# Recurrent attention and a four-branch network on one core: the order of VectorE's queue in the last group, and of two attention steps

## The chip, the core and the metric

The kernel runs on one core of a Trainium2 chip. Its time is the device time of one execution in microseconds (us); the number that counts is the median of the runs of one kernel. A profile comes from one execution of its own, so the time of that execution stands beside it.

## What is computed

Two parts follow each other. The first is a gated linear recurrence over 768 positions, for 4 batches and 8 heads of 48 numbers:

```python
for t in range(S):
    state = alpha[:, :, t, :, None] * state + np.einsum('bhd,bhe->bhde', k[:, :, t], v[:, :, t])
    y[:, :, t] = np.einsum('bhd,bhde->bhe', q[:, :, t], state)
```

Its result, seen as x with 3072 rows of 384 numbers, goes through four branches of two layers, weighted with normalised probabilities p:

```python
for e in range(E):                      # E = 4, hidden width F = 1024
    h = np.maximum(x @ w1[e], 0.0)
    out += p[:, e:e + 1] * (h @ w2[e])
```

All of it is in 32-bit floats.

## The kernel before

**Attention.** The recurrence is computed in blocks of 128 positions. There are 24 units, (block, batch) with the block as the slow index. For a unit, `attention(u)` is a Python generator; each `yield` ends a step, and the steps are issued one at a time between other work. Its steps, called beats: three steps that transpose alpha, keys and queries on TensorE (`tp`); three levels of a doubling scheme, in which ScalarE copies queries into `qb` (`copy_q`, line 307) and keys (L325), and VectorE multiplies queries and keys by decays (L314, L326); the fourth query copy, with the start of `near` on VectorE (L359); 64 score products on TensorE (`sc`, L333), taken into `near` by VectorE (L343); the last levels; the products of the far half (`far`, L388) and of two more levels; ScalarE's copies of `far` (L401) and of `near` (L405) into `lat`; then the result `yps` (L425), which multiplies the past state and `lat`, and its copy by ScalarE into `x_raw` (L441, or L445 in the last group); then the transposes of the last keys (`tp` again) with ScalarE's copy of them (L450); last, the update of the state `st` (products L454, VectorE L462 and L463) and the load of the values `v` two units ahead on the SP queue. Units of the last block (the last four) need no state update.

**The two layers.** The 24 units form seven groups: groups 0 and 6 (`LAST`) hold two units, the others four. A group's rows are columns of the first layer: 512 for four units, 256 for two. For each branch e of a group, `up` makes eight tiles of the hidden layer, and `down` the second layer. From group 1 on the products are split: a number is written as a sum of parts of fewer bits (top, low and a combination of them), and three products of parts stand for one product. In groups 2 to 6 a tile of `up` is nine matmuls into two PSUM tiles, `one` (six) and `two` (three). ScalarE takes `one` out with a factor (`t`, L538); VectorE adds `two` (L540, "the sum"); `hidden_parts` then has ScalarE make the top part with the ReLU (L563, "top"), VectorE the low part L (L565) and from both the part D (`make_dif`, L573) in two halves: the first at once, the second put into the list `later`. The generator of a tile waits in the list `finish`, and is run after the matmuls of the next tile are issued and before that tile's L538 and L540. `down` in these groups takes two units at a time: 48 products of 384 columns, first all that use top and L (32), then those that use D (16); one entry of `later` is made after every fifth product. Each unit's two sums are accumulated by VectorE (L641, the first branch by ScalarE, L639). The PSUM tiles `one`, `two` and the sums share four buffers; `tp`, `yps` and the state's products share two others; `t` has two buffers.

**The order.** [...]The tasks are (group, branch), and groups 5 and 6 take turns within each branch. Within a task, `advance` moves a clock of estimated TensorE time by the cost of each tile or product; `deal` gives each attention step a due time on that clock, and a step is issued when the clock has reached it. A unit's steps lie between a beginning and an end, two spaces long, so that two units overlap; a space is 11.5 in group 1, and 27 to 34 later. The 17 steps stood at equal distances (`BEATS = 17`). The last unit of a group ends 6.0 (`MARGIN`) before the second layer in which `split_x` takes its result. The two units of group 0 are issued by a list written out by hand. Weights are split into parts in the first two groups (L223 to L229), stored to memory on the POOL queue (L230), and loaded again on SP (L194).

Of the kernel before, what the change touches and what calls it, by code (L numbers as in the profile page):

```python
# [10 lines left out]
F32 = mybir.dt.float32  # L11
F32R = mybir.dt.float32r
# [8 lines left out]
def kernel(  # L21
# [124 lines left out]
    BEATS = 17  # L146
# [121 lines left out]
    def attention(u):  # L268
# [143 lines left out]
        yps = ps.tile([P, KC, P], F32, name="yps", tag="w")  # L412
        for c in range(KC):


            if c < 2:
                now = [[(2 * c + j // 2, j % 2, (0, HD + TAIL)[j % 2], 2 * QUAD * (j % 2))
                        for j in range(4)]]
                turns = ([(True, now[0])] if cb > 0 else []) + [(False, now[0])]
            else:  # L420
                turns = [(True, [(p, 0, 0, QUAD) for p in range(NP)])] if cb > 0 else []
                turns += [(False, [(p, i, QUAD + TAIL * i, 0) for p in range(NP)]) for i in range(2)]
            for n, (past, turn) in enumerate(turns):
                for j, (p, i, in_v, in_st) in enumerate(turn):
                    nc.tensor.matmul(  # L425
                        yps[QUAD * j:QUAD * (j + 1), c, :],
                        lhsT=flat_st[:, p, in_st:in_st + QUAD] if past
                        else flat_v[:, p, in_v:in_v + QUAD],
                        rhs=QT[:, p, :] if past else lat[:, 2 * p + i, :],
                        start=(n == 0), stop=(n == len(turns) - 1))  # L430
        gi, slot = place[cb, b]
        if slot == 0:
            if gi == 0:
                xTs[gi] = work.tile([P, 3, KC, NT], F32R, name="xT", bufs=1)
                xraws[gi] = xTs[gi][:, 2].bitcast(F32)
            elif gi < LAST:
                xraws[gi] = work.tile([P, KC, NT], F32, name="x_raw", bufs=1)
            else:
                xraws[gi] = []
        if gi < LAST:  # L440
            nc.scalar.copy(out=xraws[gi][:, :, slot * P:(slot + 1) * P], in_=yps)  # L441
        else:

            xraws[gi].append(AT)
            nc.scalar.copy(out=AT[:, :KC, :], in_=yps)  # L445
        yield

        if cb < NCB - 1:
            KB = AT
            nc.scalar.copy(out=KB, in_=turned(lambda p: KT[:, p, :]))  # L450
            yield
# [42 lines left out]
    def up(gi, e, fc, slots=None):  # L494
# [31 lines left out]
        else:  # L526
# [7 lines left out]
            while finish:  # L534
                for _ in finish.popleft():
                    pass
            t = work.tile([P, NT], F32, name="t")[:, :n]
            nc.scalar.activation(out=t, in_=one, func=ACT.Copy, scale=FINE)  # L538
            if split2(gi, e):
                nc.vector.tensor_add(t, t, two)  # L540
                finish.append(hidden_parts(t, parts))
            else:
                nc.vector.tensor_add(whole, t, two)  # L543
                finish.append(rectified(whole))
# [16 lines left out]
    def hidden_parts(x, parts):  # L561
        top, low, dif = parts
        nc.scalar.activation(out=top, in_=x, func=ACT.Relu, scale=TRIM)  # L563
        yield
        nc.vector.scalar_tensor_tensor(out=low, in0=x, scalar=0.0, in1=top.bitcast(F32),  # L565
                                       op0=ALU.max, op1=ALU.subtract)

        n = x.shape[-1]
        make_dif(*(part[:, :n // 2] for part in parts))
        later.append([part[:, n // 2:] for part in parts])  # L570
# [9 lines left out]
    def down(gi, e, slots, between):  # L580
# [14 lines left out]
        for n, (part, i, fc) in enumerate(steps):  # L595
# [7 lines left out]
            if later and n % 5 == 4:  # L603
                make_dif(*later.popleft())
# [54 lines left out]
    def deal():  # L659
# [14 lines left out]
        for gis in [*([gi] for gi in range(1, LAST - 1)), [LAST - 1, LAST]]:  # L674
# [6 lines left out]
            for k in range(n):  # L681
# [5 lines left out]
                events += [(begin + (end - begin) * (j + 1) / BEATS, u, run) for j in range(BEATS)]  # L687
# [103 lines left out]
```

## Time and profile before

| what | us |
|---|---|
| median of 12 runs | 1084.27 |
| lowest and highest of them | 1082.58, 1085.38 |
| the profiled execution | 1085.0 |
| its span on the core | 1083.2 |
| busy: TensorE, its weight loads, VectorE, ScalarE | 1058.0, 898.9, 779.7, 564.4 |

In the lines of the profile, L607 is a line of the kernel, PE is TensorE's matmuls, PEld its weight loads (which run beside the matmuls), DVE VectorE, ACT ScalarE, and SP and POOL the engines whose queues issue most transfers. `t<-one` means that the instruction writes tile `t` from tile `one`. In the timeline a line has its start, its duration, the engine, the line, the operation, the tiles, the shape and how many instructions were merged; a bracket at the end gives the idle time of the engine before it and what ended that. In the lines of waits, the numbers are the total, how often and the longest. The median time of one instruction is longer than the distance to the next one where instructions overlap in an engine's pipeline.

### The profile page before, as it was taken

The page shows a single profiled execution, that of the slowest core. Times are in us where ns is not written, and L with a number is a line of the kernel's source. Part 1 is how long each engine was busy: PE and PEld are TensorE (multiplying, and loading weights), DVE is VectorE, ACT ScalarE, POOL GpSimd, SP SyncE. Part 2 cuts the span into 40 slices and gives each one's busy share as a digit, 9 for nine tenths or more (in the row PEclk, how much of TensorE's full clock was granted, in tenths as well). Part 3 has the DMA queues.
Part 4 walks back from the last instruction along what each step waited for, and adds up shares of the span by engine and source line. Part 5 has one row for each costly group of instructions (what it writes and reads, how often), then busy time and mean ns, then how long its engine had stood idle before and what let it go on. Part 6 is the DMA issues. An engine that isn't in the chain of part 4 may idle for free.

```text
span 1083.2 us, 21627 instructions
## 1 busy us (share of the span) xinstructions
PE 1058.0 (98%) x8460; PEld 898.9 (83%) x8460; DVE 779.7 (72%) x1743; ACT 564.4 (52%) x1202; POOL 32.9 (3%) x71
## 2 busy tenths in 40 slices
PE   8889899999999999999999999999999999999998
PEld 8766677676777798898898898888989889898987
DVE  5578678657557869778878777986887965756565
ACT  5786776664757555546546445565464442323232
POOL 2000000000000100000000000000000000000000
PEclk9999999999999999999999999999999999999999
DMA  8597679796696968658759559577594444444530
GB/s 124 156 327 232 210 244 377 291 329 234 213 311 221 400 203 286 269 165 310 252 175 359 204 185 351 181 265 262 148 357 180 186 190 175 175 180 170 202 163 30
DMA packets 158838, 251.67 MB, mean 232 GB/s; under 512 B 120112, under 2 KB 135344, under 8 KB 136208
## 3 DMA queue, kind: packets, MB, share of 16 engines
q1 hardware_dynamic: 149600, 208.82, 55.8%
q0 software_dynamic: 5760, 41.29, 9.7%
q8 instruction: 67, 1.10, 0.4%
q10 hardware_dynamic: 3376, 0.17, 0.3%
q14 instruction: 35, 0.29, 0.1%
HBM read 207.79 MB, written 42.47 MB: 231 GB/s over the span
## 4 chain that ended last, share of the span: by engine, by line
PE 78%; DVE 9%; ACT 7%; issue 3%; DMA 2%; SPq 0%; ACTq 0%; DVEq 0%
PE ops L607 25%; PE one L531 19%; PE ops L611 9%; PE two L531 9%; PE sc L333 5%; PE yps L425 3%; PE tp L265 2%; ACT qb L307 2%; DVE t L540 2%; PE one L523 2%; DVE hT L565 2%; ACT hT L563 2%; PE sps L454 1%; PE far L388 1%; DVE near L343 1%
## 5 line engine op out<-in xcount | busy, mean ns | idle before, releaser
L607 PE MATMUL ops<-w,hT 128*128 128x384 f32 x1728 | 318.3, 340 | 2.0 <-DVE acc L641 1.5
L607 PEld LDWEIGHTS ops<-w,hT 128*128 128x128 f32 x1728 | 298.7, 188 | 7.8 <-DVE acc L641 2.8
L531 PE MATMUL one<-xT,w 128*128 128x512 f32 x960 | 253.7, 399 | 1.1 <-DMA w<-kept 0.7
L531 PEld LDWEIGHTS one<-xT,w 128*128 128x128 f32 x960 | 175.8, 188 | 42.4 <-issue 2.4
L538 ACT ACTIVATE t<-one 128x512 f32<-128x512 f32 (+1 forms) x192 | 106.1, 553 | 162.0 <-PE one L531 145.7
L307 ACT COPY qb<-QT 64x256 f32<-64x256 f32 x336 | 136.6, 406 | 70.0 <-DVE QT L288 35.7
L563 ACT ACTIVATE hT<-t 128x512 fp32r<-128x512 f32 (+1 forms) x160 | 94.3, 590 | 122.5 <-DVE t L540 121.3
L565 DVE SCALAR_TENSOR_TENSOR hT<-t,hT 128x512 fp32r<-128x512 f32 (+1 forms) x160 | 102.3, 639 | 75.5 <-ACT hT L563 74.1
L531 PE MATMUL two<-xT,w 128*128 128x512 f32 x480 | 136.2, 392 | 0.0
L611 PE MATMUL ops<-hT 128*128 128x384 f32 x384 | 135.6, 497 | 0.0
L573 DVE SCALAR_TENSOR_TENSOR hT<-hT 128x256 fp32r<-128x256 f32 (+1 forms) x320 | 117.4, 395 | 5.5
L540 DVE TENSOR_TENSOR t<-t,two 128x512 f32<-128x512 f32 (+1 forms) x160 | 100.7, 629 | 23.6 <-PE two L531 11.7
L531 PEld LDWEIGHTS two<-xT,w 128*128 128x128 f32 x480 | 90.2, 188 | 19.8
L611 PEld LDWEIGHTS ops<-hT 128*128 128x128 f32 x384 | 70.0, 192 | 40.5 <-issue 1.6
L343 DVE COPY_PREDICATED near<-masks,sc 128x256 f32<-128x256 uint8 x144 | 77.1, 535 | 17.9 <-PE sc L333 14.8
L314 DVE TENSOR_TENSOR QT<-QT,dec 128x256 f32<-128x256 f32 x144 | 60.7, 422 | 33.1 <-ACT qb L307 32.7
L333 PEld LDWEIGHTS sc<-qb,KT 128*64 128x64 f32 x2304 | 72.5, 138 | 9.2 <-issue 7.1
L333 PE MATMUL sc<-qb,KT 128*64 128x64 f32 x2304 | 76.7, 223 | 0.2 <-ACT qb L307 0.2
L641 DVE SCALAR_TENSOR_TENSOR acc<-ops,p_all,acc 128x384 f32<-128x384 f32 x82 | 49.5, 613 | 29.1 <-PE ops L607 13.7
L326 DVE TENSOR_TENSOR KT<-KT,dec 128x256 f32<-128x256 f32 x144 | 60.3, 419 | 2.6 <-PE tp L265 2.6
L325 ACT COPY KT<-KT 128x256 f32<-128x256 f32 x144 | 59.8, 416 | 3.1
L543 DVE TENSOR_TENSOR hT<-t,two 128x512 f32<-128x512 f32 x32 | 22.0, 688 | 35.6 <-ACT t L538 26.1
(88 smaller groups left out, 972.3 us busy)
## 6 DMA issues: line engine op xcount, KB each, us to landing
w<-kept SPq DMA_DIRECT2D x144, 1152.0 KB
kept<-w POOLq DMA_DIRECT2D x32, 1152.0 KB, 7.6
hT<-in_moe_w_dram SPq DMA_DIRECT2D x32, 384.0 KB
w<-in_moe_w_dram SPq DMA_DIRECT2D x48, 128.0 KB
ra<-in_alpha_dram SPq DMA_DIRECT2D x23, 192.0 KB
rk<-in_k_dram SPq DMA_DIRECT2D x23, 192.0 KB
rq<-in_q_dram SPq DMA_DIRECT2D x23, 192.0 KB
out_dram<-acc POOLq DMA_DIRECT2D x18, 192.0 KB, 5.8
```

Of the source, the lines that this page charges most:

```text
L307: nc.scalar.copy(out=qb[rows, :, i, :].rearrange("p a (b r) -> p a b r", r=m), in_=qv[rows])
L314: nc.vector.tensor_mul(qv, qv, spread(dv[:, :, :, 0], m))
L333: nc.tensor.matmul(out[HALF * s:HALF * (s + 1), 2 * p:2 * p + 2, :], lhsT=KTs[li][:, p, HALF * s:HALF * (s + 1)], rhs=qbs[li][:, p, :, QUA ...
L343: nc.vector.copy_predicated(near.rearrange("p a (b two r) -> p a b two r", two=2, r=m)[:, :, :, 1, :], mk.unsqueeze(1).broadcast_to([P, H, ...
L531: nc.tensor.matmul(out, lhsT=w[:, part, kc], rhs=x_part(gi, part, kc), start=(part == terms[0] and kc == 0), stop=(part == terms[-1] and k ...
L538: nc.scalar.activation(out=t, in_=one, func=ACT.Copy, scale=FINE)
L540: nc.vector.tensor_add(t, t, two)
L563: nc.scalar.activation(out=top, in_=x, func=ACT.Relu, scale=TRIM)
L565: nc.vector.scalar_tensor_tensor(out=low, in0=x, scalar=0.0, in1=top.bitcast(F32), op0=ALU.max, op1=ALU.subtract)
L573: nc.vector.scalar_tensor_tensor(out=dif, in0=top.bitcast(F32), scalar=1 / 4096.0, in1=low.bitcast(F32), op0=ALU.mult, op1=ALU.subtract)
L607: nc.tensor.matmul(sums[i][part // 2], lhsT=h[:, part], rhs=w, start=(fc == 0 and part != 1), stop=(fc == FCH - 1 and part != 0))
L611: nc.tensor.matmul(sums[i][0], lhsT=h[:, 2].bitcast(F32), rhs=w, start=(fc == 0), stop=(fc == FCH - 1))
```

## The change

There are five edits.

1. The beats become a list: eleven at distances of 0.055 of a unit's time (before, 1/17 = 0.0588), then 0.69, 0.75, 0.80, 0.87, 0.94 and 1.0 (before, 0.706, 0.765, 0.824, 0.882, 0.941 and 1.0).
2. From unit 2 on, the transposes of the last keys and ScalarE's copy of them (`turn_keys`) are issued one step before the result and its copy (`result`) instead of one step after. Units of the last block have an empty step in the place of `turn_keys`, so their result moves from step 15 to step 16 and the load of `v` from step 16 to step 17.
3. In the last group, only the top part of the tile before is issued ahead of a tile's L538 and L540. Its L (L565) is issued behind that L540.
4. In the last group no half of D is made in `up`: the whole part, 256 columns, goes into `later`.
5. `down` makes one entry of `later` after every fourth product instead of every fifth.

```diff
-    BEATS = 17
+    BEATS = [*(0.055 * (j + 1) for j in range(11)), 0.69, 0.75, 0.8, 0.87, 0.94, 1.0]
...
+        def result():
+            yps = ps.tile([P, KC, P], F32, name="yps", tag="w")
...
+        def turn_keys():
+            if cb < NCB - 1:
+                nc.scalar.copy(out=AT, in_=turned(lambda p: KT[:, p, :]))
+
+
+        for step in (turn_keys, result) if u >= half else (result, turn_keys):
+            step()
+            yield
 
         if cb < NCB - 1:
             KB = AT
-            nc.scalar.copy(out=KB, in_=turned(lambda p: KT[:, p, :]))
-            yield
...
-            while finish:
-                for _ in finish.popleft():
+
+            ends_first = gi < LAST
+            for steps in finish:
+                for _ in steps if ends_first else [next(steps)]:
                     pass
+            ahead = [] if ends_first else list(finish)
+            finish.clear()
             t = work.tile([P, NT], F32, name="t")[:, :n]
             nc.scalar.activation(out=t, in_=one, func=ACT.Copy, scale=FINE)
             if split2(gi, e):
                 nc.vector.tensor_add(t, t, two)
+                for steps in ahead:
+                    next(steps, None)
                 finish.append(hidden_parts(t, parts))
...
         n = x.shape[-1]
-        make_dif(*(part[:, :n // 2] for part in parts))
-        later.append([part[:, n // 2:] for part in parts])
+        at = n // 2 if n == NT else 0
+        if at:
+            make_dif(*(part[:, :at] for part in parts))
+        later.append([part[:, at:] for part in parts])
...
-            if later and n % 5 == 4:
+            if later and n % 4 == 3:
                 make_dif(*later.popleft())
...
-                events += [(begin + (end - begin) * (j + 1) / BEATS, u, run) for j in range(BEATS)]
+                events += [(begin + (end - begin) * beat, u, run) for beat in BEATS]
```

## The prediction

> **What bounds the kernel now.** I read the page first (TensorE busy 98% of the span), then the chain that ended last (78% TensorE, 9% VectorE, 7% ScalarE), then TensorE's waits, then the stretches and the timeline where the chain leaves TensorE. The busy time by stretch, columns PE, PEld, DVE, ACT, POOL, then clock, DMA share, GB/s:
>
> ```profile
> 60.00:150.00 90.00, 80.91 (x858) 61.61 (x857) 66.02 (x151) 64.29 (x145) 4.80 (x9) 0.96 0.72 234
> 150.00:180.00 30.00, 29.09 (x179) 21.06 (x178) 24.82 (x49) 20.38 (x43) 3.22 (x6) 1.00 1.04 396
> 180.00:700.00 520.00, 518.33 (x4154) 430.48 (x4156) 385.05 (x838) 287.15 (x593) 15.01 (x28) 1.00 0.73 260
> 700.00:903.00 203.00, 201.85 (x1735) 179.82 (x1725) 158.09 (x361) 104.04 (x223) 2.16 (x4) 1.00 0.61 220
> 903.00:1083.00 180.00, 174.74 (x984) 159.67 (x983) 112.33 (x263) 51.11 (x114) 0.00 (x0) 1.00 0.42 165
> ```
>
> From 180 to 903 us TensorE has under 3 us without work: nothing that only moves VectorE's or ScalarE's work can gain there. It lacks 9 us at 60–150 and 5 us at 903–1083. What it waits for (total, times, longest):
>
> ```profile
> PE yps L425 <- ACT lat L405: 8.5, 6, 3.5
> PE far L388 <- ACT qb L307: 4.6, 4, 1.6
> PE ops L607 <- DVE acc L641: 1.5, 2, 0.9
> ```
>
> The two long waits on `lat` lie at 77.7 and 120.8, and a stretch at half clock follows each (the 0.50 column), with TensorE busy all through it:
>
> ```profile
> 80.84:84.25 3.41, 3.41 (x34) 1.99 (x22) 2.96 (x6) 3.17 (x8) 0.00 (x0) 0.50 0.31 107
> 125.21:128.62 3.41, 3.41 (x28) 2.03 (x21) 1.96 (x6) 1.51 (x4) 0.00 (x0) 0.50 0.88 341
> ```
>
> The other place is the last group's first layer, four times eight tiles of 256 columns. Its timeline:
>
> ```profile
> 903.90 0.88 PE L531 MATMUL one<-KT,w 128*128 128x256 f32 x6
> ...
> 904.98 0.88 PE L531 MATMUL one<-KT,w 128*128 128x256 f32 x6
> ...
> 907.37 0.41 DVE L540 TENSOR_TENSOR t<-t,two 128x256 f32<-128x256 f32 x1
> ...
> 907.82 0.42 ACT L563 ACTIVATE hT<-t 128x256 fp32r<-128x256 f32 x1 [0.88 <-DVE t L540]
> ...
> 908.14 0.37 ACT L538 ACTIVATE t<-one 128x256 f32<-128x256 f32 x1
> 908.27 0.42 DVE L565 SCALAR_TENSOR_TENSOR hT<-t,hT 128x256 fp32r<-128x256 f32 x1 [0.48 <-ACT hT L563]
> 908.56 0.77 PEld L531 LDWEIGHTS one<-KT,w 128*128 128x128 f32 x6 [0.30 <-ACT t L538]
> ...
> 908.73 0.29 DVE L573 SCALAR_TENSOR_TENSOR hT<-hT 128x128 fp32r<-128x128 f32 x1
> 908.94 0.41 DVE L540 TENSOR_TENSOR t<-t,two 128x256 f32<-128x256 f32 x1
> ...
> 913.26 8.59 PE L607 MATMUL ops<-w,hT 128*128 128x384 f32 x48
> ```
>
> Unhindered, TensorE starts a tile every 904.98 − 903.90 = 1.08 us. VectorE's sums (L540) come every 908.94 − 907.37 = 1.57 us, because sum, top (L563), L (L565), D (L573) and the next sum follow one another. After three tiles PSUM is full and TensorE keeps VectorE's pace.
>
> **What the Trainium skill says.** *Perfetto Trace Analysis*, Identifying the Most-Contended Engine: matmul busy time is a poor measure of the distance to the limit. The trace agrees: PE reads 98% while the last group's tiles run at 1.57 instead of 1.08 us; so I count starts, not busy time. *TensorE: Matmul & The Clock Gate*, Part 1: an idle window of about 3.4 us halves the clock until a busy window has passed. The trace agrees, with 3.41 us at 0.50 twice, after waits of 2.73 and 3.50 us. *VectorE: DVE Perf Modes*, the section on the fixed latency of SBUF operations: (N+151)/0.96 ns for an fp32 tensor-tensor operation, 424 ns at N = 256; the trace has 415 (L540) and 425 (L565). I use the trace.
>
> **The change, part by part.**
>
> *Last group, first layer.* VectorE's queue becomes sum(k), L(k−1), sum(k+1); D leaves. The loop that remains is sum(k) → top(k) → t(k+1), behind top(k) in ScalarE's queue → sum(k+1): 907.82 − 907.37 = 0.45, then 908.14 − 907.82 = 0.32, then eviction to sum 0.42 (903.80 to 904.22 at the stage's first tile): 1.19 us. The new wait: t(k+1) also needs the `t` buffer that L(k−1) reads. L follows a sum after about 0.345 us (nine 256-column pieces in 3.11 us at 890.00) and is heard by ScalarE after 0.45, so t starts 0.80 after the sum: 1.22 us. I take 1.22. That is above 1.08, but two tiles of PSUM lie between: t(k) starts at 903.80 + 1.22k and frees its bank 0.42 later (908.14 → 908.56), so tile k may start at 901.78 + 1.22k and wants 902.84 + 1.08k. They meet at k = 7.6: only the second layer waits, 0.06 us. The layer takes 8 × 1.08 + 0.06 = 8.70 instead of 913.26 − 902.84 = 10.42, and 4 × 1.72 = **6.9 us** go. Bounds: 2.6 (loop 1.40) to 7.1 (no stop).
>
> *D in the second layer.* Eight pieces of 256 replace two sets of eight of 128, at about 0.345 against 2 × 0.21 us each. The last L ends some 2.6 us after the second layer begins, so the pieces are through 8 × 0.345 = 2.8 later, at 5.4. The first is needed at product 32 (32 × 0.179 = 5.7; 48 products take 8.59), then one per product; the eighth, emitted before product 31 behind one accumulation (0.62), is due at 7.0 and done at about 6.5. TensorE hides it: 0, at most 0.3 each. In groups 2 to 5 the same pieces come at every fourth product instead of every fifth: seven instead of five stand ahead of the first accumulation, 0.7 us, and its bank is wanted 18 products = 3.2 us later. 0, −1 to +1 us.
>
> *Keys ahead of the result, and the beats.* Four transposes and a ScalarE copy (0.58 us) go ahead of the result's products and their copy (0.48), which come a beat later; the state update keeps its beat. The keys need VectorE's last L326, done at 76.1 where the turn comes at 77.4, and at 119.4 where it comes at 120.4. In the first attention group two units overlap at a beat of 23/17 = 1.35 us, and ScalarE, 64 of 90 us busy, is late for each copy.
> At 77.4 the copy of `near` moves ahead of one first-layer tile's work (0.38 + 0.84), so `lat` is ready at 79.2 instead of 80.4. But the next unit's score products now follow the result at once and need a query copy that ScalarE ends at 83.3 either way. They end at 83.9 and one product behind them at 84.25; before, both were through at 86.3: 2.1 us.
> At 120.4 the earlier first beats put a query copy into ScalarE's idle 1.9 us at 116.7, `lat` is ready at 122.9, and the scores end at 126.6, a product later 126.95, at full clock; before, that point was reached at 132.0: 5.0 us. At 99.5 the wait of 0.96, some 1.2 with what follows, goes. Sum 8.3. Behind it, at 150–180, VectorE (24.8 of 30) and the DMA (1.04) are full; their work is issued earlier too, but not all will follow. I take **6**. Bounds: 0, since ScalarE does the same work, and 12.5 = 1.6 (far) + 7.4 (lat) + 2 × 3.41/2 (clock).
> In later groups the result is about 2 us or more behind its copies already; one wait (0.87 at 804.97) goes: **1.0**, bounds −1 and 2. The loads of `v` for the last two units leave one beat (3 us) later on SP, over 20 us ahead of use: 0. The result must be there for the split of x: 0.06 of two spaces of 27–34 us plus a margin of 6 leaves 9 us. 0.
>
> *Sum:* 6.9 + 6 + 1 = 13.9. The profiled run took 1085.0 (span 1083.2 and 1.8 around it), 0.7 above the median of 1084.27. Against the median: 1084.3 − 13.9 = **1070.4**.
>
> **Rivals.**
> 1. *ScalarE sets the pace at 60–150 in any order*: TensorE no longer waits for `lat` but for the query copies behind it. For it: ScalarE is never idle at 77.7–84. Against: it idles 1.9 us at 116.7 and at 127. Only the last group's gain and 1 us stay: 1084.3 − 7.9 = 1076.4.
> 2. *The last group's loop is longer*, 1.40: the two hand-overs from L and top to t add up. Tile 8 then waits until 912.6; each layer saves 0.65: 1084.3 − 2.6 − 7 = 1074.7.
> 3. *Slower*: the D pieces and denser first beats delay VectorE's accumulations, so that each second half of a second layer waits for its banks. There are 16 such places in groups 2–5. It decides once the delay passes the 3.2 us of slack; at 1.1 us each it costs 17.6: 1084.3 − 13.9 + 17.6 = 1088.0. For it: two such waits today. Against: they total 1.5 us, and the added backlog is 0.7.
> 4. *All waits at 60–150 go*, with the clock: 1084.3 − 6.9 − 12.5 = 1064.9.
>
> **How the numbers follow.** Forecast 0.56, rivals 0.20, 0.12, 0.04, 0.06; rivals 1 and 2 together (2.6 + 1) with 2 us lost to the beats elsewhere, 0.02: 1082.7, which is no change. The range leaves out the slower one and the far end of rival 4: 1065.0 to 1078.5, where 1078.5 is rival 1 with −1 us elsewhere and a few tenths more. A measurement of this kernel can tell about 0.2% (2.2 us) from no change. All other cases but the slower one lie beyond that: faster 0.94, same 0.02, slower 0.04.
>
> **What would show it.** First layers of the last group at about 8.7 us with L540 every 1.2 us; no waits of the result on `lat` above 1.5 us; no half-clock stretches at 80–130; 180–700 unchanged within 2 us. I am wrong if TensorE's wait only moves to the scores (L333) or to the key transposes (L265), or if waits on the accumulations (L641) grow past 5 us.

## The result and the profile after

| | before | after |
|---|---|---|
| median, us | 1084.95 (32 runs) | 1073.26 (8 runs) |
| lowest and highest, us | 1082.58, 1087.15 | 1072.18, 1075.76 |
| the profiled execution and its span, us | 1085.0, 1083.2 | 1074.11, 1072.3 |

The ratio of after to before is 0.9897, with a 95% interval of 0.9888 to 0.9906. The median fell by 11.7 us, the profiled span by 10.9; 13.9 were forecast. The line numbers of the changed kernel are higher: L308 is the copy of queries, L334 the scores, L389 `far`, L402 and L406 the copies into `lat`, L428 the result, L540 the first layer's products, L551, L553, L578, L580 and L590 are t, sum, top, L and D, L624 and L628 the second layer's products, L658 the accumulation, and L248 the split of x.

The busy times by stretch of the changed kernel (the columns are those of the prediction's table); the last two stretches are moved along with the work:

```profile
60.00:150.00 90.00, 84.80 (x897) 67.10 (x896) 70.44 (x162) 71.41 (x158) 5.56 (x11) 1.00 0.80 263
150.00:180.00 30.00, 27.88 (x195) 19.91 (x194) 24.02 (x50) 18.01 (x40) 2.68 (x5) 0.94 1.01 361
180.00:700.00 520.00, 518.98 (x4215) 433.91 (x4214) 387.97 (x844) 287.41 (x592) 14.99 (x28) 1.00 0.74 262
700.00:895.00 195.00, 190.85 (x1607) 171.06 (x1597) 151.50 (x345) 98.87 (x213) 2.16 (x4) 1.00 0.60 214
895.00:1073.00 178.00, 173.47 (x999) 161.56 (x997) 107.88 (x232) 54.24 (x115) 0.00 (x0) 1.00 0.42 167
```

At 60–150 TensorE lacks 5.2 us where it lacked 9.1, and its clock is full. At 150–180 something new has come: 2.1 us without work instead of 0.9, and a clock of 0.94. And 700–895 now lacks 4.2 us where the like stretch lacked 1.2. TensorE's waits in the changed kernel (total, times, longest) say on what:

```profile
PE ops L624 <- DVE acc L658: 4.4, 4, 1.9
PE far L389 <- ACT qb L308: 3.2, 3, 1.6
PE yps L428 <- ACT lat L406: 3.1, 4, 1.5
PE sc L334 <- ACT qb L308: 2.6, 3, 1.2
PE one L540 <- DVE xT L248: 1.3, 1, 1.3
...
PE one L540 <- DMA w<-kept: 0.8, 1, 0.8
```

The result's wait on `lat` fell from 8.5 to 3.1 us. The scores (L334), the accumulations (L658) and the split of x (L248) wait longer than before.

To see where time came from, I took the start of the same product on TensorE in both traces and subtracted:

| first product of | before | after | saved so far |
|---|---|---|---|
| group 0, branch 3, second layer | 157.80 | 150.73 | 7.07 |
| group 1, branch 0, first layer | 171.90 | 165.13 | 6.78 |
| group 1, branch 1, first layer | 220.60 | 215.84 | 4.77 |
| group 4, branch 1, second layer | 762.23 | 754.58 | 7.66 |
| group 4, branch 2, first layer | 783.31 | 777.41 | 5.90 |
| group 6, branch 0, first layer | 902.84 | 897.34 | 5.49 |
| the end | 1083.22 | 1072.35 | 10.88 |

So 7.1 us are won by 150 us, 2.3 of them are lost again by 216 us, 0.7 net come by 897 (2.9 won by 755, of which 1.8 go in one layer and 0.4 later), and 5.4 in the last stretch. The four first layers of the last group took 9.03 us each, where they had taken 10.42, 10.42, 10.71 and 10.43: 1.39 + 1.39 + 1.68 + 1.40 = 5.9 us.

The last group's first layer in the timeline of the changed kernel (a bracket gives the engine's idle time before the line, and what ended it):

```profile
1053.26 0.42 DVE L553 TENSOR_TENSOR t<-t,two 128x256 f32<-128x256 f32 x1 [0.76 <-ACT t L551]
...
1053.60 0.42 DVE L580 SCALAR_TENSOR_TENSOR hT<-t,hT 128x256 fp32r<-128x256 f32 x1
1053.71 0.42 ACT L578 ACTIVATE hT<-t 128x256 fp32r<-128x256 f32 x1 [0.49 <-DVE t L553]
...
1054.13 0.39 ACT L551 ACTIVATE t<-one 128x256 f32<-128x256 f32 x1
...
1054.55 0.42 DVE L553 TENSOR_TENSOR t<-t,two 128x256 f32<-128x256 f32 x1 [0.53 <-ACT t L551]
```

VectorE's queue is sum, L of the tile before, sum. The distance of two sums is 1054.55 − 1053.26 = 1.29 us (it was 1.57, and 1.22 was forecast). ScalarE's t starts 1054.13 − 1053.71 = 0.42 after top, not 0.32 behind it: it waits for something other than ScalarE's queue.

In the second layer after it, the D pieces in VectorE's timeline of the changed kernel:

```profile
1062.24 2.43 DVE L590 SCALAR_TENSOR_TENSOR hT<-hT 128x256 fp32r<-128x256 f32 x7
...
1065.86 0.42 DVE L590 SCALAR_TENSOR_TENSOR hT<-hT 128x256 fp32r<-128x256 f32 x1
```

That layer begins at 1059.72, so the eighth piece is done 1066.28 − 1059.72 = 6.56 us after it (about 6.5 was worked out, 7.0 was due). TensorE does not wait for it.

The two places of attention, on TensorE in the changed kernel:

```profile
80.17 1.08 PE L428 MATMUL yps<-lat,rv 128*32 128x128 f32 x32 [1.17 <-ACT lat L406]
81.18 1.65 PE L334 MATMUL sc<-qb,KT 128*64 128x64 f32 x48
84.04 0.69 PE L334 MATMUL sc<-qb,KT 128*64 128x64 f32 x16 [1.21 <-ACT qb L308]
84.66 1.56 PE L628 MATMUL ops<-hT 128*128 128x384 f32 x4
```

```profile
121.30 0.43 PE L428 MATMUL yps<-lat,rv 128*32 128x128 f32 x8 [1.45 <-ACT lat L406]
```

The waits on `lat` were 2.73 and 3.50 us here; they are 1.17 and 1.45, and a wait of the scores on a query copy (1.21) stands behind the first. Nothing runs at half clock. The stretch that does is a new one, on TensorE of the changed kernel at 165–171:

```profile
165.13 0.71 PE L540 MATMUL one<-xT,w 128*128 128x512 f32 x2 [0.82 <-DMA w<-kept]
167.14 1.79 PE L540 MATMUL one<-xT,w 128*128 128x512 f32 x4 [1.30 <-DVE xT L248]
```

```profile
167.49:170.90 3.41, 3.41 (x12) 2.72 (x11) 1.45 (x3) 1.69 (x4) 0.55 (x1) 0.50 1.00 423
```

Group 1's first tile waits for reloaded weights (0.82), runs two products, and waits 1.30 us for the third split of x. On VectorE seven instructions of the next attention units, from L285 to the two of L344, stand between the second and the third split (L248):

```profile
163.79 0.55 DVE L285 TENSOR_TENSOR t<-rq,rk 128x384 f32<-128x384 f32 x1
...
165.60 0.88 DVE L344 COPY_PREDICATED near<-masks,sc 128x256 f32<-128x256 uint8 x2
166.40 0.68 DVE L248 TENSOR_TENSOR xT<-x_raw,xT 128x512 fp32r<-128x512 f32 x1
```

**The clock, execution by execution.** Each run gives its span and the mean clock granted over it. One stretch of 3.41 us at half clock takes 3.41 / 2 / 1083 = 0.0016 off that mean, and costs 3.41 / 2 = 1.7 us where TensorE is busy. The kernel before is listed here by the 22 runs that were made beside the first four experiments (their median is 1084.24):

| kernel | spans at 1.000 | at 0.998 | below |
|---|---|---|---|
| before (22 runs) | none | 11: 1081.0 to 1082.4 | 11: 1082.5 to 1084.9 |
| after (9 runs) | 4: 1070.4 to 1071.2 | 4: 1071.8 to 1072.3 | 1: 1074.0 |

The same program is granted a different number of such stretches in different executions. *TensorE: Matmul & The Clock Gate*, Part 1, of the Trainium skill says that the window which the gate watches runs freely, and that the number of slow matmuls at a kernel's start therefore differs from run to run. The runs here show that the number of later half-clock stretches differs too; that it does so for this reason is not shown. At equal clock (0.998, middle values 1081.5 and 1072.2) the change is worth 9.3 us. The rest, 1.7 us against 1084.24 and 2.4 against 1084.95, goes with half-clock stretches that happen less often.

### The profile page after: what moved, and what is told of

Read it like the earlier page. It is cut to its first block, busy times and chain, and to the rows that moved or that the text cites. A ratio compares the mean times of both kernels' runs of the same rounds, so it can differ in the third digit from the quotient of the medians.

```text
span 1072.3 us, 21614 instructions
## 1 busy us (share of the span) xinstructions
PE 1048.7 (98%) x8460; PEld 899.9 (84%) x8460; DVE 775.1 (72%) x1711; ACT 567.2 (53%) x1202; POOL 32.8 (3%) x71
## 4 chain that ended last, share of the span: by engine, by line
PE 83%; DVE 8%; ACT 6%; issue 2%; DMA 1%; SPq 0%; DVEq 0%; ACTq 0%
PE ops L624 25%; PE one L540 21%; PE ops L628 10%; PE two L540 10%; PE sc L334 6%; PE yps L428 3%; PE tp L266 3%; PE one L532 2%; ACT qb L308 2%; PE far L389 1%; PE sps L463 1%; DVE near L344 1%; DVE t L553 1%; DVE hT L580 1%; DVE hT L590 1%
## 5 line engine op out<-in xcount | busy, mean ns | idle before, releaser
L624 PE MATMUL ops<-w,hT 128*128 128x384 f32 x1728 | 318.2, 340 | 4.5 <-DVE acc L658 4.4
L624 PEld LDWEIGHTS ops<-w,hT 128*128 128x128 f32 x1728 | 299.7, 188 | 9.7 <-DVE acc L658 5.7
L540 PE MATMUL one<-xT,w 128*128 128x512 f32 x960 | 254.1, 400 | 2.6 <-DVE xT L248 1.3
L540 PEld LDWEIGHTS one<-xT,w 128*128 128x128 f32 x960 | 176.4, 189 | 42.0 <-DVE xT L248 1.7
L551 ACT ACTIVATE t<-one 128x512 f32<-128x512 f32 (+1 forms) x192 | 106.5, 555 | 154.1 <-PE one L540 148.9
L308 ACT COPY qb<-QT 64x256 f32<-64x256 f32 x336 | 136.6, 406 | 76.7 <-DVE QT L289 44.0
L578 ACT ACTIVATE hT<-t 128x512 fp32r<-128x512 f32 (+1 forms) x160 | 94.3, 589 | 123.3 <-DVE t L553 122.6
L580 DVE SCALAR_TENSOR_TENSOR hT<-t,hT 128x512 fp32r<-128x512 f32 (+1 forms) x160 | 102.2, 639 | 55.6 <-ACT hT L578 53.8
L540 PE MATMUL two<-xT,w 128*128 128x512 f32 x480 | 136.9, 394 | 0.0
L628 PE MATMUL ops<-hT 128*128 128x384 f32 x384 | 133.4, 491 | 0.0
L553 DVE TENSOR_TENSOR t<-t,two 128x512 f32<-128x512 f32 (+1 forms) x160 | 100.9, 630 | 42.0 <-ACT t L551 22.9
L590 DVE SCALAR_TENSOR_TENSOR hT<-hT 128x256 fp32r<-128x256 f32 x288 | 111.9, 421 | 4.4
L540 PEld LDWEIGHTS two<-xT,w 128*128 128x128 f32 x480 | 90.6, 189 | 20.1
L628 PEld LDWEIGHTS ops<-hT 128*128 128x128 f32 x384 | 69.5, 190 | 40.1 <-issue 0.6
L344 DVE COPY_PREDICATED near<-masks,sc 128x256 f32<-128x256 uint8 x144 | 76.9, 534 | 15.5 <-PE sc L334 12.8
L334 PEld LDWEIGHTS sc<-qb,KT 128*64 128x64 f32 x2304 | 72.7, 138 | 9.7 <-issue 5.6
L334 PE MATMUL sc<-qb,KT 128*64 128x64 f32 x2304 | 77.2, 223 | 2.6 <-ACT qb L308 2.6
L658 DVE SCALAR_TENSOR_TENSOR acc<-ops,p_all,acc 128x384 f32<-128x384 f32 x82 | 49.5, 613 | 34.0 <-PE ops L624 14.6
L558 DVE TENSOR_TENSOR hT<-t,two 128x512 f32<-128x512 f32 x32 | 22.0, 688 | 35.6 <-ACT t L551 24.4
```

The source lines that it names most:

```text
L308: nc.scalar.copy(out=qb[rows, :, i, :].rearrange("p a (b r) -> p a b r", r=m), in_=qv[rows])
L334: nc.tensor.matmul(out[HALF * s:HALF * (s + 1), 2 * p:2 * p + 2, :], lhsT=KTs[li][:, p, HALF * s:HALF * (s + 1)], rhs=qbs[li][:, p, :, QUA ...
L344: nc.vector.copy_predicated(near.rearrange("p a (b two r) -> p a b two r", two=2, r=m)[:, :, :, 1, :], mk.unsqueeze(1).broadcast_to([P, H, ...
L540: nc.tensor.matmul(out, lhsT=w[:, part, kc], rhs=x_part(gi, part, kc), start=(part == terms[0] and kc == 0), stop=(part == terms[-1] and k ...
L590: nc.vector.scalar_tensor_tensor(out=dif, in0=top.bitcast(F32), scalar=1 / 4096.0, in1=low.bitcast(F32), op0=ALU.mult, op1=ALU.subtract)
L624: nc.tensor.matmul(sums[i][part // 2], lhsT=h[:, part], rhs=w, start=(fc == 0 and part != 1), stop=(fc == FCH - 1 and part != 0))
```

## The experiments

My theory after the result: edits 3 and 4 give the 5 to 6 us of the last group and are held at 1.29 us by the two buffers of `t`; the keys turned early (edit 2) give the rest; the beats (edit 1) and edit 5 give nothing by themselves. Rivals: the beats cost or win something; edit 5 costs waits in groups 2 to 5; the gain of attention is only the clock; ScalarE sets the pace. The first four kernels ran beside a kernel before at 1084.24 (median), the next four beside 1084.57, the last four beside 1084.98.

### The last group alone

```diff
 # edits 3, 4 and 5 on the kernel before
+            ends_first = gi < LAST
...
-            if later and n % 5 == 4:
+            if later and n % 4 == 3:
```

> The kernel before with the last group's part alone (edits 3, 4 and 5). My theory: the two parts of the change act in different stages and add up. The four first layers of the last group shrink by 1.4 to 1.7 us each, as in the changed kernel's trace (9.03 instead of 10.42), so 5.9 us less than before, about 1079.0; nothing changes ahead of 890 us. Rival: part of the last group's gain comes from TensorE arriving there earlier after the attention edits; then it is under 4 us. Second rival: one D piece per four products costs time in groups 2 to 5; then the second layers grow and it is under 5 us.

Measured: 1080.25 us, ratio 0.9958 [0.9944, 0.9971]; that is 4.6 less by the ratio (3.1 to 6.1), and 4.0 between the medians. In its trace each of the four first layers saves 1.39 or 1.40, 5.6 together. Up to 102 us this trace gains 1.6, where the edits change nothing: a half-clock stretch fewer. From there to 505 us, through the first three branches of group 2, no layer gains or loses more than 0.1. From 505 to 903 it loses 1.0, and the waits on the accumulations are 2.8 us in this trace, 1.5 before. The loss lies in three second layers: 0.3 at 505 (the last of group 2), 0.2 at 632 and 0.7 at 848 (the last of group 4). So the second rival, a cost of edit 5, is in part right, and its sign (under 5 us) came; as a cost in each of many places it falls.

### The early keys alone

```diff
 # edit 2 on the kernel before
+        for step in (turn_keys, result) if u >= half else (result, turn_keys):
+            step()
+            yield
```

> The kernel before with the order of result and key transposes alone (edit 2), beats still at equal distances. My theory: what matters is that the result comes a beat after its copies, so most of the attention gain is here: 3 to 5 us less than before, with the two waits on lat of 2.7 and 3.5 us at 77 and 121 us cut to about half. Rival: the gain comes from the beats, which put the query copies into ScalarE's gaps; then this one stands within 1.5 us of before.

Measured: 1077.03 us, ratio 0.9929 [0.9916, 0.9941], 7.2 less, more than expected. The waits in its trace:

```profile
PE yps L426 <- ACT lat L405: 4.6, 4, 2.3
PE far L388 <- ACT qb L307: 4.4, 4, 1.6
```

The start of group 0's last second layer is 6.3 us earlier than before, and its whole trace has no half-clock stretch: 3 of 5 runs had a clock of 1.000, where none of the kernel before had. Of the 7.2 about 2 to 3 are thus the clock's; the rest is the order. The one run at 0.998 has a span of 1076.2, which is 5.3 less than the middle value of the kernel before at that clock.

### The beats alone

```diff
-    BEATS = 17
+    BEATS = [*(0.055 * (j + 1) for j in range(11)), 0.69, 0.75, 0.8, 0.87, 0.94, 1.0]
```

> The kernel before with the list of beats alone (edit 1), the result still ahead of the key transposes, so that it now falls at 0.87. My theory: little, 0 to 2 us less than before, since the result still follows its last copy by 0.07 of a unit instead of 0.0588; the wait of far on the query copy goes (1.6 us), the waits on lat stay over 2 us each. Rival: the beats alone bring the 5 us.

Measured: 1083.3 us (18 runs), ratio 0.999 [0.9983, 0.9997], about 1 less. Its waits:

```profile
PE yps L425 <- ACT lat L405: 6.6, 5, 3.1
...
PE one L531 <- DVE xT L247: 2.0, 1, 2.0
```

The wait on `lat` loses 1.9 us, that on the split of x gains 1.8 (it was 0.2). At a clock of 0.998 its spans are 1081.0 to 1081.9 (12 runs), the same as before. The tenth of a per cent goes with the clock: of its 18 runs 3 are at 1.000 and 3 below 0.998, of the 22 before none and 11. Its trace is one of the three; by 158 us it is 4.1 us ahead of the kernel before, of which two half-clock stretches fewer make 3.4.

### Keys and beats together

```diff
 # edits 1 and 2 on the kernel before
```

> The kernel before with both attention edits (1 and 2) and nothing of the last group's part. My theory: the changed kernel less its last group's gain, 5 us less than before, about 1080.0, and the stage at 164 to 171 us loses about 2 us of what was gained up to there, with TensorE at half clock for 3.4 us, as in the changed kernel. If the two parts were not additive, this one and the last group's part alone would not sum to the whole (10.3 per cent of a per cent: 1.03% of the time) within 1 us.

Measured: 1078.54 us, ratio 0.9945 [0.9931, 0.9958], 5.7 less. With the last group alone (4.0) that makes 9.7, against 11.0 for the whole against 1084.24; the intervals cover the difference. Beside the early keys the beats win nothing. Two half-clock stretches fell into this trace, at 167.63 (after the waits on weights and on the split of x) and at 764.96, after the longest of these waits:

```profile
PE ops L614 <- DVE acc L648: 3.0, 2, 1.9
```

The wait of 1.9 us is in the changed kernel too, at 765.10; it is 0.9 with the keys alone, 1.2 with keys and equal beats, and absent from the kernel before and from the last group alone.

### A third buffer for t

```diff
-            t = work.tile([P, NT], F32, name="t")[:, :n]
+            t = work.tile([P, NT], F32, name="t", bufs=3)[:, :n]
```

This and the next kernels start from the changed kernel (here the other tile of that name gets three buffers too).

> The changed kernel with three buffers for t instead of two. In the changed kernel's last group a sum follows the last one after 1.29 us where I had worked out 1.22. My theory: the eviction into t waits for L of two tiles before, which now stands behind a sum, and that hand-over takes 0.53 us and not the 0.45 that I took. With a third buffer the wait is gone and ScalarE's own order decides: sums every 1.19 us, first layers of 8.7 us instead of 9.03, 4 times 0.3 = 1.2 us less than the changed kernel. Rival: the time is ScalarE's, whose eviction starts when the top part ends (0.42 after its start) and not after 0.32; then the sums stay at 1.29 and the time doesn't move.

Measured: 1071.97 us, ratio to before 0.9883 [0.9866, 0.99]. The same place in its timeline:

```profile
1053.07 0.42 DVE L553 TENSOR_TENSOR t<-t,two 128x256 f32<-128x256 f32 x1 [0.42 <-ACT t L551]
...
1053.53 0.42 ACT L578 ACTIVATE hT<-t 128x256 fp32r<-128x256 f32 x1 [0.49 <-DVE t L553]
...
1053.85 0.37 ACT L551 ACTIVATE t<-one 128x256 f32<-128x256 f32 x1
...
1054.25 0.42 DVE L553 TENSOR_TENSOR t<-t,two 128x256 f32<-128x256 f32 x1 [0.42 <-ACT t L551]
```

Now t follows top at once (0.32) and the sums come every 1.18 us. The first layers take 8.63 us, TensorE's own pace. So in the changed kernel t did wait for L to release its buffer, and that wait is 4 × 0.40 = 1.6 us of time. The theory holds. (The medians differ by 1.3, less than their intervals can tell apart; the traces show the 1.6.)

### The third split of x earlier

```diff
-                    for step, at in enumerate((0.0, 0.52, 0.62, 0.72)):
+                    for step, at in enumerate((0.0, 0.52, 0.62, 0.68 if gi == 0 else 0.72)):
```

> The changed kernel with the third split of x for group 1 issued a product earlier (0.68 instead of 0.72 of the second layer), so that VectorE makes it ahead of the next unit's fifth query level and not behind it. In the changed kernel TensorE waits 1.3 us there for that split, then runs 3.41 us at half clock, and 2.3 us of what was gained by 150 us is lost by 215 us. My theory: this wait is what the new beats brought, and it also brings the half clock; without it TensorE starts the second k-part about 1.3 us earlier, stays at full clock, and the kernel is 1.5 to 2.5 us faster than the changed one. Rival: the weights' DMA (0.8 us of waiting, transfers at full share) holds the place next; then it is within 0.7 us of the changed kernel and the half-clock stretch stays.

Measured: 1070.99 us, ratio 0.9876 [0.9862, 0.9891]. In its trace the wait on the split is gone, nothing runs at half clock at 165–180, and 2.04 us are saved between 165 and 187. So what was lost at that place was the split of x behind attention's work on VectorE, plus the half-clock stretch that followed the two waits. The wait on the weights stays (1.00), and a new one of 0.88 us on VectorE's L558, at 170.85, takes back part of the 1.3 + 1.7. This trace lost 1.7 us again at 763, where the old wait on the accumulations was followed by half clock:

```profile
762.51 3.92 PE L624 MATMUL ops<-w,hT 128*128 128x384 f32 x12 [1.89 <-DVE acc L658]
```

```profile
762.74:766.15 3.41, 3.41 (x12) 3.29 (x11) 2.99 (x8) 0.00 (x0) 0.00 (x0) 0.50 0.00 0
```

### TensorE kept busy in the kernel before

```diff
         yps = ps.tile([P, KC, P], F32, name="yps", tag="w")
+        for _ in range(10 if u in (2, 4) else 0):
+            nc.tensor.matmul(yps[:, 0, :], lhsT=ident, rhs=ident, start=True, stop=True)
```

Ten products of no use fill the wait ahead of two results, in the old order; their sums are overwritten.

> The kernel before with ten matmuls of no use (128 columns each, overwritten by the result's own) ahead of the results of units 2 and 4, in the place of the waits of 2.7 and 3.5 us at 77 and 121 us. The waits stay, TensorE is not idle in them. My theory: part of what the attention edits gained is the clock: with it kept up, two stretches of 3.41 us at half clock go, 1.7 us each at most, so 2 to 3 us less than before, without any change to ScalarE's or VectorE's order. Rival: ScalarE sets the pace behind those waits, and a full clock only makes TensorE wait elsewhere: within 0.7 us of before.

Measured: 1082.35 us (15 runs), ratio 0.9979 [0.9972, 0.9987], 2.2 less. Of its runs 11 had a clock of 1.000 and 3 of 0.999, and at 60–150 the trace shows full clock:

```profile
60.00:150.00 90.00, 85.30 (x917) 67.40 (x916) 67.88 (x154) 67.30 (x150) 4.79 (x9) 1.00 0.76 247
```

Its trace is 3.4 us ahead of the kernel before from 143 us on, two half-clock stretches of 1.7. A kernel that does more work on TensorE is faster because the clock does not drop. The clock alone is worth these 2.2 us, less what the products themselves cost; it isn't the 7.2 of the early keys.

### A ScalarE step moved to GpSimd

```diff
-        nc.scalar.activation(out=dif, in_=whole, func=ACT.Copy, scale=TRIM * 4096)
+        nc.gpsimd.tensor_scalar_mul(out=dif, in0=whole, scalar1=TRIM * 4096)
```

> The changed kernel with the second step of each weight split (one of ScalarE's two, 32 of 128x768 in all) given to GpSimd instead. It takes 16 operations of 0.84 us from ScalarE between 60 and 165 us. If ScalarE sets TensorE's pace there in the changed kernel (5.2 us of 60 to 150 are without work on TensorE), 2 to 4 us go. If latency and order do, and not ScalarE's load, it is within 1 us, or slower where VectorE now waits for GpSimd (an operation that takes over 2 us there delays the splits and their stores, and the loads of group 1 at 165 us).

Measured: 1087.5 us, ratio to before 1.0029 [1.0019, 1.0039], some 14 slower than the changed kernel. One of the two groups of this line in its trace, and the same group in the trace of the changed kernel (busy, mean ns; then idle before):

```profile
L226 POOL TENSOR_SCALAR w<-w 128x768 fp32r<-128x768 f32 x16 | 34.6, 2163 | 14.0 <-DMA w<-in_moe_w_dram 12.8
...
L226 ACT ACTIVATE w<-w 128x768 fp32r<-128x768 f32 x16 | 13.5, 841 | 0.1
```

GpSimd takes 2.16 us for what ScalarE does in 0.84, and VectorE then waits for it (28.0 us in 14 waits, up to 3.4). Its trace also has 17.1 us at half clock in four places, where that of the changed kernel has 3.4; up to (17.1 − 3.4) / 2 = 6.8 us of the difference are the clock's. ScalarE has less to do and the kernel is slower, but because something else has become late. Whether ScalarE sets the pace is not told apart by this.

### The changed kernel with equal beats

```diff
-    BEATS = [*(0.055 * (j + 1) for j in range(11)), 0.69, 0.75, 0.8, 0.87, 0.94, 1.0]
+    BEATS = [(j + 1) / 17 for j in range(17)]
```

> The changed kernel with the beats at equal distances again (edits 2 to 5 without 1). The run with the key transposes alone was 7.2 us less than before, with both attention edits 5.7 less, so I now hold that the beats cost about 1.5 us on top of the other edits: they bring the wait on the split of x at 167 us, and put more of an attention unit's VectorE work into one second layer, whose accumulations then come late (1.9 us of waiting and a half-clock stretch near 762 us in two of the traces). Then this one is 1 to 2.5 us faster than the changed kernel, about 1071.3. Rival: the two medians differ by the chance of half-clock stretches only, and the last group's part needs the beats; then it is within 0.7 us of the changed kernel.

Measured: 1073.74 us, ratio 0.9897 [0.9882, 0.9912], the same as the changed kernel. The theory that the beats cost 1.5 us beside the early keys falls: what the early keys alone had over both together was the number of half-clock stretches in the runs (at 0.998 the spans are 1076.2 with the keys alone, 1075.8 and 1076.8 with both). Its own trace shows the chance of it. It is the program of the early keys alone up to the last group but for edit 5, and the wait of the result on `lat` that ends near 80.5 is 2.3 us in both, but here the clock dropped after it:

```profile
81.41:84.82 3.41, 3.41 (x40) 2.11 (x34) 3.38 (x7) 2.69 (x7) 0.16 (x1) 0.50 0.33 110
```

### Equal beats and three buffers

```diff
 # both edits: BEATS as (j + 1) / 17, and bufs=3 for t
```

> The same with three buffers for t. The third buffer took the last group's sums from 1.29 to 1.18 us apart and 1.3 us from the changed kernel's time. My theory: it acts in another stage than the beats, so the two add up: about 1070, 3 to 4 us less than the changed kernel.

Measured: 1071.78 us, ratio 0.9879 [0.9864, 0.9893]: 2.0 below the kernel with two buffers and equal beats. The third buffer gives its 1.6 again. The 1070 that was expected counted on a gain of the equal beats that does not exist.

### D after every fifth product again

```diff
-            if later and n % 4 == 3:
+            if later and n % 5 == 4:
```

> The changed kernel with one D piece per five products instead of four (edit 5 undone). In the last group the eighth piece is then issued right before product 39, which is the one that reads it, and the last two stand behind both units' first accumulations (0.62 us each) on VectorE. My theory: product 38 or 39 waits 0.3 to 0.6 us in each of four second layers, so 1 to 2.5 us more than the changed kernel, about 1075; in groups 2 to 5 nothing. Rival: the denser pieces of edit 5 delay the accumulations in groups 2 to 5; then this one is faster than the changed kernel.

Measured: 1073.92 us, ratio 0.9902 [0.9887, 0.9917], by time not to be told from the changed kernel. In the trace it is: each of the last three second layers of the last group is 0.5 us longer (0.56, 0.56, 0.49), and this is where, in its timeline:

```profile
1064.98 1.14 DVE L658 SCALAR_TENSOR_TENSOR QT<-ops,p_fine,QT 128x384 f32<-128x384 f32 x2 [0.90 <-PE ops L624]
1066.04 0.75 DVE L590 SCALAR_TENSOR_TENSOR hT<-hT 128x256 fp32r<-128x256 f32 x2
1066.51 0.19 PEld L624 LDWEIGHTS ops<-w,hT 128*128 128x128 f32 x1 [0.50 <-DVE hT L590]
```

Two pieces are left behind the accumulations and come 0.5 too late. Edit 5 is what lets edit 4 be free. The first of the four is 0.15 shorter. Against the changed kernel, group 2 does not move, and three second layers, at 583 (group 3), 710 and 842 (group 4), win 0.5, 0.2 and 0.3. That is as much as the last group alone lost, not at the same layers. So edit 5 takes 1.0 and gives 0.56 + 0.56 + 0.49 − 0.15 = 1.5. The wait of 1.9 on the accumulations in group 4 is still there, with a half-clock stretch after it: it isn't edit 5's.

### What looked best, together

```diff
 # the changed kernel with equal beats, bufs=3 for t, eight useless products
 # ahead of the results of units 2 and 4, and
-                    for step, at in enumerate((0.0, 0.52, 0.62, 0.72)):
+                    for step, at in enumerate((0.0, 0.52, 0.62, 0.625 if gi == 0 else 0.72)):
```

> The version that the experiments point to: the changed kernel with equal beats, three buffers for t, the third split of x for group 1 in the place of the second one's product (0.625), and eight matmuls of no use ahead of the results of units 2 and 4, so that TensorE isn't idle while it waits for lat. My theory: every part acts in its own place, and the clock no longer drops: 1068 to 1070, 3 to 5 us faster than the changed kernel. Rival: without the beats the clock doesn't drop anyway and the split isn't late, so that the last two parts bring nothing (within 0.7 us of the version with equal beats and three buffers).

Measured: 1071.86 us (1069.67 to 1072.53), ratio 0.9873 [0.9856, 0.989]. All its four runs had a clock of 1.000, and the spans are still 1067.9 to 1070.8. It is no faster than the third buffer alone or the early split alone, so the gains do not add. With equal beats alone the wait on the split is 0.2 us in the trace, so there was little to win by an earlier split. The useless products take time of their own, and this trace has a wait of 1.7 us on a load of weights (`hT<-in_moe_w_dram`) that no other here has at that length. How the loss divides between these is not shown.

**The clock taken out.** A run's span times its mean clock is an estimate of its span at full clock, worked out from the runs. It takes TensorE to be busy at half clock, as it is in the stretches shown, and the clock is listed to 0.001, so a single value is good to about 0.5 us. The middle values:

| kernel | estimate, us |
|---|---|
| before; the same with useless products | 1079.2; 1080.5 |
| beats alone; keys alone; both | 1079.4; 1074.4; 1074.6 |
| last group alone | 1075.1 |
| the changed kernel; with equal beats | 1070.2; 1069.8 |
| with three buffers; with equal beats too | 1068.0; 1068.3 |
| with the early split; with every fifth product | 1068.8; 1070.9 |
| what looked best, together | 1070.1 |

By this the last group's part (4.1) and attention's (4.6) make 8.7 of the whole's 9.0, the beats give nothing, and twenty useless products cost 1.3 us where the clock isn't at stake.

## Why the prediction was right, and where its sizes were off

The direction, the places and the order of sizes held; 1073.26 lies within 1065.0 to 1078.5. The sum was 2.9 us too high against 1084.27 as the start (3.0 in the traces).

| step | forecast | trace |
|---|---|---|
| last group's first layers | 6.9 | 5.9 |
| D in the second layer | 0 | −0.5 in the last group; −1.0 in groups 2 to 4 (within the row of later groups) |
| attention at 60–150, what is left by 216 us | 6 | 7.1 − 2.3 = 4.8 |
| later groups | 1.0 | 0.7 |
| sum | 13.9 | 10.9 |

Part of the agreement is chance. The forecast started from an execution with two half-clock stretches, and the one profiled afterwards had one. At equal clock the change is worth 9.0 to 9.3 us; the rest of the 11.7 is the number of stretches, which differs from run to run. One sum of the prediction is off: its bound of 12.5 takes 7.4 for the waits on `lat` at 60–150, which total 2.73 + 3.50 + 0.96 = 7.2, and its terms then make 12.2. Rival 4 would stand at 1065.2; nothing else hangs on it.

**The last group's loop** is right in its mechanism and wrong in one term. I took 0.45 for the time from the start of L to the moment when ScalarE may write its buffer, the hand-over that I had measured between sum and top. It is 1054.13 − 1053.60 = 0.53. The other term is the distance from a sum to L, 0.34 as forecast. A loop of 1.29 instead of 1.22 seems nothing, but it decides whether PSUM's two spare tiles last for eight tiles: at 1.22 only 0.06 us were to be left of the wait, at 1.29 it is 0.40 per layer. The third buffer takes this hand-over out of the loop, and 1.18 is then within 0.01 of the 1.19 that I had worked out without L. Rival 2 (1.40) named the right place with too high a price. The third layer's saving of 1.68 is not a different mechanism; that layer was longer before.

**D in the second layer** is done in time in the last group, as worked out. Still the four second layers there are 0.15, 0.06, 0.07 and 0.18 us longer than before: TensorE waits for nothing in them, but its products stand a little farther apart (in the last one the 37th starts 6.46 us after the first, 6.35 before, and 6.35 again with edit 5 undone). Why is open; it lies within the 0.3 each that was allowed for.

**The early keys** did what the working said, somewhat less of it. By 102 us 2.1 + 1.2 were worked out and 2.8 came; at 120 it was 5.0 and 3.9 came. The scores at 77–84 were to end at 83.9; they ended at 84.7, because the last 16 of them waited 1.21 us for the query copy that I had named, which ScalarE ended 0.7 us later than the 83.3 that I had taken. The waits and the clock account for the sum: 84.80 − 80.91 = 3.9 us more of busy TensorE, and two half-clock stretches fewer (3.4) make 7.3, where 7.1 were saved by 150 us. By the kernel with the early keys alone (6.3 at that point) this is edit 2's; what the beats add there, 0.7, is gone by 216 us, and they have no part in the whole that could be measured.

**What followed it** was foreseen in kind and not in place. I took 6 of 8.3, since VectorE and the DMA are full at 150–180. What was lost there is 2.3 us, and the early split, which wins back 2.04, shows that it is VectorE's third split of x behind seven instructions of attention, and a half-clock stretch after it. I had costed the split of x at nothing, with 9 us of margin for the result that it reads (for group 1, with its spaces of 11.5, it is 0.06 × 23 + 6 = 7.4); the result was there in time, but VectorE's queue was not. That step failed: the cover that I checked was the data's, not the engine's that has to work on it.

**The accumulations** wait 4.4 us instead of 1.5, close to the 5 at which I said that I would be wrong. The third rival named this wait; its mechanism, the denser D pieces, costs the 1.0 us of edit 5 (I took 0, with −1 to +1 as the bounds), not 17.6. The largest wait, 1.9, came with attention's new order: 0.9 of it with the keys alone, and none with edits 3 to 5 alone. It lies in group 4, on TensorE of the changed kernel:

```profile
754.58 8.64 PE L624 MATMUL ops<-w,hT 128*128 128x384 f32 x48
765.10 2.35 PE L624 MATMUL ops<-w,hT 128*128 128x384 f32 x12 [1.89 <-DVE acc L658]
767.38 0.42 PE L428 MATMUL yps<-QT,st 128*32 128x128 f32 x8
```

In the kernel before, the result's products lay ahead of the last six of those 48:

```profile
762.23 7.55 PE L607 MATMUL ops<-w,hT 128*128 128x384 f32 x42
769.72 0.43 PE L425 MATMUL yps<-QT,st 128*32 128x128 f32 x8
...
771.59 5.13 PE L607 MATMUL ops<-w,hT 128*128 128x384 f32 x28
```

That gave VectorE 771.59 − 769.72 = 1.9 us for its accumulations before the 49th product wanted a bank. Now the 48 run through until 763.2, VectorE's first accumulation starts at 764.44, and the result follows 12 products later, when it covers nothing. That accumulation also comes later within its layer: 764.44 − 754.58 = 9.9 us after the layer's start, where it was 771.01 − 762.23 = 8.8. I had not followed the moved result to the layers in which it lands.

**The clock** was in the forecast as two stretches that go. They did go in this trace, and one came at 167. Over many runs the kernel before has one or more in each, the changed one none or one in nearly all. What the mean clock lacks, times the span, is 3.3 us on average in the 22 runs before and 1.4 in the nine after: 1.9 us. The filled kernel shows 2.2 us for the clock less the cost of its products. I had taken the waits of 2.73 and 3.50 us as agreeing with an idle window of about 3.4 us. As a rule for a single wait the runs do not bear that out: one of 3.15 us had no half-clock stretch after it (the beats alone, at 122), nor one of 2.73 (the last group alone, at 80), and one of 1.89 had (the early split, at 763).

**Rival 1** (ScalarE sets the pace) had its sign: the scores now wait 2.6 us for query copies. But at 60–150 the sum of the waits on `lat`, `far` and the scores fell from 7.2 + 1.6 + 0.2 = 9.0 to 2.6 + 0 + 2.6 = 5.2. So ScalarE's pace took part of the gain and not all of it. How much more a faster ScalarE would give stays open: the one kernel that was to tell it moved the work to an engine that was too slow for it. Also open is which of the waits of 1 to 3 us drops the clock in a given execution.

## What to carry to other kernels

When a step is taken out of a loop of two engines, add the hand-over of every buffer that the loop reuses, and measure that hand-over as such: it was 0.08 us longer than that of a result, and a third buffer was worth 1.6 us. When a step is moved, follow it to where it lands: it may have been the cover of another engine's work. Before a difference of 1 to 3 us is put down to an edit, look at the granted clock of every run; two programs of the same speed differ by 1.7 us for each half-clock stretch.

## What the hardware did that I had not expected

- Waits as short as 0.82 and 1.30 us with two products between them were followed by a half-clock stretch of 3.41 us (at 167), and one of 1.89 us in some executions (763) and not in others (765 in the changed kernel's trace). In the trace before, only those of 2.73 and 3.50 us had shown it; with the beats alone a wait of 3.15 us was followed by none.
- More work made a kernel faster: ten products of no use at two places, 2.2 us less.
- The release of a buffer by VectorE's L was heard by ScalarE 0.53 us after its start, while the result of VectorE's sum was used 0.45 after its start, though both instructions last 0.42 us.
- A scaling of 128x768 fp32 numbers took 2.16 us on GpSimd and 0.84 on ScalarE.
